# Weights in smaller loads, and a new order of stages, in an adaLN attention-and-GEGLU kernel

## The chip, the cores and the metric

The kernel runs on one core of one Trainium2 chip. The metric is the device time of one execution in microseconds (us). A profile of one execution, taken by the hardware profiler, goes with each kernel; the times in it are microseconds from the start of its span.

A few names that the profile uses: PE is TensorE (matmuls), PEld its weight loads, DVE is VectorE, ACT is ScalarE, POOL is GpSimd and SP is SyncE, which here only issues transfers. "SPq" is SP's queue of transfer issues. L681 is line 681 of the kernel.

## What is computed

One transformer block with adaptive layer norm, for 2048 tokens of width 512, in bfloat16:

```python
mod = (silu(c) @ w_mod)                      # six rows of 512: sa, ca, ga, sb, cb, gb
h = layernorm(x) * (1 + ca) + sa
x = x + ga * A(h, wqkv, wo)                  # attention
h = layernorm(x) * (1 + cb) + sb
x = x + gb * ((gelu(h @ w_gate) * (h @ w_up)) @ w_down)    # width 1792 inside
```

The attention has 32 heads of width 16. A token sees 8 tokens: itself and those 2, 4, ... 14 places before it. The softmax is over these eight.

## The kernel before

**Tiling.** The tokens go through in five groups, `GROUPS`: two of 256 tokens and three of 512. For each group the stages are: layer norm and transposition into `hT` (`ln1`), the projections to Q, K and V (`emit_qkv`, matmuls at L681, copies out of PSUM at L704), attention (`emit_attention`), a second layer norm into `h2T`, and the feed-forward part (`emit_ffn`, gate and up matmuls at L945, down matmuls at L971). The feed-forward of a group is emitted after the attention of the next one.

**Attention without a score matrix.** Q times the shifted K is an elementwise product on VectorE (`pq`, L764), which a narrow matmul folds over a head's width into `LT` (L776). The maximum over the eight is found on VectorE (`Lb`, L797 to L819) and subtracted by a matmul (L824). Exp on ScalarE gives `e` (L831). Two matmuls with the constant F1 sum `e` over the eight places into `ss` (L839). ScalarE turns the sum into its reciprocal by Ln and Exp (L844, L845), and VectorE multiplies (L848). `e` times the shifted V is again a product on VectorE (`pv`, L860 and L866), folded by matmuls into `o_ps` (L879). The shifted V comes from memory: V is stored to a scratch tensor (`scr`, L708) and read back shifted as `vR` (four transfers for each tile, L725). The output projection with `woP` is at L904. VectorE has multiplied `woP` by the row ga once, at L999, after all four of its loads, and `WdP` by gb at L1002.

**Loads.** All large loads are issued from SP. `load_rows` cuts a weight into `cuts` transfers of equal size; before the change w_gate (`Wg`), w_up (`Wu`) and w_down (`WdP`) come in two halves each. `load_wqkv` loads a third of wqkv; wq comes in two halves, wk and wv whole. The first group's K projection is written in two steps for each PSUM tile, rows 0 to 255 of wk and then rows 256 to 511; in the built program both tiles take their first step before either takes its second.

**What sets the order.** No order is written out by hand. Every operation is recorded with an engine, an estimated time, the tiles that it reads and writes, and a priority from the table `PRI`. `Plan.order` then places operations one by one: of those that are ready, it takes the one with the earliest start by its own estimate of times, and among equals the lowest priority. `Plan.MARGIN` adds a margin for each engine, `Plan.AHEAD` holds loads back that are not urgent, and `Plan.SKEW` adds to the estimated end of a transfer in a long run of transfers. `emit` writes the instructions in the order so found, and each engine runs its own in that order. So a change of a number in `PRI` can move instructions on any engine.

Each transfer is given one of eight completion counters in turn, and an issue on SP waits until the transfer eight places before it is complete.

Of the kernel before, what the change touches and what calls it, by code (L numbers as in the profile page):

```python
# [8 lines left out]
ACT = mybir.ActivationFunctionType  # L9
ALU = mybir.AluOpType  # L10
AX = mybir.AxisListType
F32 = mybir.dt.float32
# [6 lines left out]
def _ap(base, free_dims, offset=0):  # L19
    return bass.AP(base.tensor, base.offset + offset, [list(base.ap[0])] + [list(d) for d in free_dims])  # L20
# [164 lines left out]
class Engines:  # L185
    def __init__(self, nc, pl):
# [14 lines left out]
MERGE = (3, 4)  # L201
FMERGE = 0
DVEMAX = (4,)
CUT = 384
XB1 = {4: "act"}
XB2 = {1: "act", 2: "act", 3: "act", 4: "act"}
PRI = {
        "mod0": 3.1,
        "ln1": (-1825.3, -1417, -559.1, -142.2, 405),
        "qkv": (-441.8, 155.6, 232.8, 131.6, 1308),  # L210
        "att": (-554.3, 44.5, -1074.5, 462.1, 1752.4),
        "ffn": (1196.5, 2593, 2774.3, 2477.6, 1886.7),
        "glu": (5.6, 211.5, -2302.6, 838.6, 2147),
        "mod": (-159.3, -303.9, 262.1),
        "wo": 1823,
        "wd": 1171.4,
        "scr": -3307.9,
        "vR": -3609.4,
        "warm": (5, 6, 0, 3),
        "load": {"wk": -997.5, "wv": -995.5, "x1": -997.86, "x2": -995.23, "wm2": -1001.63, "wo": -878.5, "x3": -1000.04,  # L220
        "wm3": -994.66, "wm4": -996.59, "x4": -995.73, "Wg": -868.86, "Wu": -870.61, "wm5": -855.38, "Wd":
        -862.75},
}
Plan.MARGIN = {"pe": 0.48, "act": -0.15, "dve": 0.16, "pool": -1.48, "sp": 0.37}
Plan.AHEAD = 2.07
Plan.SKEW = 2.6
Plan.TURN = 0


# [1 line left out]
def kernel(  # L231
# [13 lines left out]
    nc = tc.nc  # L245
    P = 128
    S, D = 2048, 512
    H, DH, W = 32, 16, 8
    F = 1792
    SG = 512  # L250
    DT = D // P
# [42 lines left out]
    F1 = ctile([P, P], BF16, "F1")  # L294
# [109 lines left out]
    def load_rows(t, src, p, cuts, rows):  # L404
        n = len(t.shape) and t.shape[1] // cuts
        for i in range(cuts):
            dma(1835e3 / cuts, lambda i=i: nc.sync.dma_start(
                out=t[:, i * n:(i + 1) * n, :],
                in_=src[i * n * P:(i + 1) * n * P, :].rearrange(rows, p=P)),
                w=[(t, k) for k in range(i * n, (i + 1) * n)], pri=p + 0.1 * i, bw=385e3)  # L410

    L = PRI["load"]
# [3 lines left out]
        w=[wm01], pri=-999, bw=390e3)  # L416

    def load_wqkv(b, p, cuts=1):
        m = DT // cuts
        for i in range(cuts):  # L420
            dma(524e3 / cuts, lambda i=i: nc.sync.dma_start(
                out=wqkv[b][:, m * i:m * i + m, :],
                in_=A_wqkv[m * i * P:m * (i + 1) * P, b * D:(b + 1) * D].rearrange("(o p) n -> p o n", p=P)),
                w=[(wqkv[b], k) for k in range(m * i, m * i + m)], pri=p + 0.02 * i)

    load_wqkv(0, -998.65, 2)
    load_wqkv(1, L["wk"])
    load_wqkv(2, L["wv"])
    load_x(2, 4, L["x1"])
    load_x(4, 8, L["x2"])  # L430
# [1 line left out]
    for d4 in range(4):  # L432
        dma(131e3, lambda d4=d4: nc.sync.dma_start(
            out=woP[32 * d4:32 * d4 + 32, :, :],
            in_=bass.AP(A_wo.tensor, A_wo.offset + 4 * D * d4, [[16 * D, H], [D, 4], [1, D]])), w=[(woP, d4)],
            pri=L["wo"], bw=250e3)
# [1 line left out]
    load_wm(wm3, 3, L["wm3"])  # L438
    load_wm(wm4, 4, L["wm4"])
    load_x(12, 16, L["x4"])  # L440
    load_rows(Wg, B_w_gate, L["Wg"], 2, "(dt p) f -> p dt f")
    load_rows(Wu, B_w_up, L["Wu"], 2, "(dt p) f -> p dt f")
    load_wm_halves(wm5, 5, L["wm5"])
    load_rows(WdP, B_w_down, L["Wd"], 2, "(dt p) f -> p dt f")

    wps = T("psF", [P, SG], F32, "warm_ps")

# [20 lines left out]
    def sigmoid():  # L468
# [6 lines left out]
        w=[scT], pri=-2000)  # L475
# [72 lines left out]
    mod0 = []  # L548
# [108 lines left out]
    q, hT, vR = {}, {}, {}  # L657
# [56 lines left out]
    def emit_attention(g):  # L714
        tok0, n = GROUPS[g]
# [5 lines left out]
        for i, t in enumerate(vR[g]):  # L721
            rs = [(scr, (gg, i if GROUPS[gg][1] == SG else 0)) for gg in range(max(g - 1, 0), g + 1)]
            for r in (0, 2, 1, 3):
                queue, on = (nc.scalar, E.dma_act) if r in SECOND else (nc.sync, dma)
                on(32 * 4 * njv * (n + 8) * 2, lambda r=r, t=t, i=i, queue=queue: queue.dma_start(  # L725
                    out=t[32 * r:32 * r + 32, :, :, :].rearrange("p a b c -> p (a b) c") if njv == 4
                    else t[32 * r:32 * r + 32, :, :, :],
                    in_=bass.AP(scr.t.tensor, scr.t.offset + 2 * i * ROW + tok0 + 2 + 2 * r,
                                [[16 * ROW, H], [ROW, 16], [1, n + 8]] if njv == 4 else
                                [[16 * ROW, H], [4 * ROW, 4], [ROW, 2], [1, n + 8]])),  # L730
                    r=rs, w=[(t, r)], pri=PRI["vR"] + 0.1 * g, bw=330e3 if SECOND else 205e3)
# [25 lines left out]
        for jj in range(steps):  # L757
            p = base + jj
            pq = products("pq", jj)
            pqs.append(pq)  # L760
            for m in range(4):
                j, wg = (2 * jj + m // 2, m % 2) if n == SG else (m, 0)
                no = 4 if n == SG else 8
                dve(1.145, lambda j=j, wg=wg, no=no, t=pq[m]: nc.vector.tensor_tensor(  # L764
                    out=t[:], in0=_ap(q[g][:, j, :], [[0, no], [1, n]]),
                    in1=_ap(kT[:, j, :], [[2, no], [1, n]], offset=tok0 + HALO - (6 + 8 * wg if no == 4 else 14)),
                    op=ALU.mult), r=[(q[g], j)] + kd(j), w=[pq[m]], pri=p)
# [14 lines left out]
        p = base + 5  # L782
# [9 lines left out]
        e = T("e", [P, 2, n], BF16, "e")  # L792
        for b in range(nb):
            act(act_us(SG), lambda b=b: nc.scalar.copy(out=Lb[:] if nb == 1 else Lb[:, b:b + 1, :], in_=LT[b][:]),
                r=[LT[b]], w=[(Lb, b)], pri=p - 1000)
        us = 0.072 + n * 0.52e-3
        dve(us, lambda: nc.vector.tensor_tensor(out=Lb[:, 0, :], in0=Lb[:, 0, :], in1=Lb[:, 1, :], op=ALU.max),  # L797
            r=[Lb], w=[Lb], pri=p)
        if g in DVEMAX:
# [12 lines left out]
            for b, t in enumerate(LT):  # L812
                dve(0.072 + SG * 2 // nb * 1.041e-3, lambda t=t: nc.vector.tensor_tensor(
                    out=t[:], in0=t[:], in1=_ap(all4[:], [[0, 2 // nb], [1, n]]), op=ALU.subtract), r=[t, all4], w=[t],
                    pri=p)
        else:
            dve(us, lambda: nc.vector.tensor_tensor(out=Lb[0:64, 1, :], in0=Lb[0:64, 0, :], in1=Lb[64:128, 0, :],
                                                    op=ALU.max), r=[Lb], w=[Lb], pri=p)
            dve(us, lambda: nc.vector.tensor_tensor(out=Lb[0:32, 0, :], in0=Lb[0:32, 1, :], in1=Lb[32:64, 1, :],  # L819
                                                    op=ALU.max), r=[Lb], w=[Lb], pri=p)  # L820
# [11 lines left out]

        act(act_us(SG) * nb, exps, r=LT, w=[e], pri=p - 1000, table="exp")

        ss = T("psB", [P, n], F32, "ss")

        def sums():
            for wg in range(2):
                nc.tensor.matmul(ss[:], lhsT=F1[:], rhs=e[:, wg, :], start=(wg == 0), stop=(wg == 1))  # L839

        pe(2 * MM * n / SG, sums, r=[F1, e], w=[ss], pri=p, pad=ss)

        def invert():
            nc.scalar.activation(out=ss[:], in_=ss[:], func=ACT.Ln)  # L844
            nc.scalar.activation(out=ss[:], in_=ss[:], func=ACT.Exp, scale=-1.0)  # L845

        act(2 * act_us(n) + 0.1, invert, r=[ss], w=[ss], pri=p - 1000, table="exp")
        dve(0.072 + 2 * n * 1.041e-3, lambda: nc.vector.tensor_tensor(  # L848
            out=e[:], in0=e[:], in1=_ap(ss[:], [[0, 2], [1, n]]), op=ALU.mult), r=[e, ss], w=[e], pri=p)

        oT = T("oT", [P, 4, SG], BF16, "oT")
        pvs = []
        for jj in range(steps):
            p = base + 6 + jj
            pv = products("pv", jj)
            pvs.append(pv)
            if n == SG:
                for m in range(4):
                    jl, wg = m // 2, m % 2
                    dve(1.145, lambda jj=jj, jl=jl, wg=wg, t=pv[m]: nc.vector.tensor_tensor(  # L860
                        out=t[:], in0=_ap(e[:, wg, :], [[0, 4], [1, n]]),
# [25 lines left out]
        p = base + 11  # L887
# [150 lines left out]
```

## Time and profile before

| what | us |
|---|---|
| median of 5 runs | 243.18 (242.39 to 243.86) |
| the profiled execution | 242.39 |
| its span | 240.4 |
| TensorE busy | 233.9 (97% of the span) |
| VectorE busy | 160.9 |
| ScalarE busy | 159.2 |
| GpSimd busy | 13.9 |

The loads before the first use of w_gate come in one stream: 28.23 MB go through the queues in all, and the first 52 us hold most of the loads. For single transfers, the time line of SP gives the moment of the issue, and the view of transfers gives the time from issue to landing:

| transfer | issued | to landing |
|---|---|---|
| wk, 512 KB | 3.67 | 7.1 |
| wv, 512 KB | 4.20 | 8.1 |
| woP, the first of four, 128 KB | 14.00 | 8.6 |
| scr store of the first group, 272 KB | 16.82 | 7.3 |
| Wu, first half, 896 KB | 19.04 | 8.2 |
| Wu, second half, 896 KB | 20.66 | 10.8 |
| vR of the first group, the first of four, 264 KB | 24.10 | 8.4 |

Busy time is not a bound by itself: an engine that is busy for most of the span can still wait in the stretch that matters. The view of waits tells for each engine what it sat idle for, and the chain that ended last follows the end of the kernel back from wait to wait.

### The profile page before, as it was taken

The numbers are of one execution on the slowest core, as the hardware profiler recorded it, in microseconds if no ns is written. First come the engines' busy times: TensorE is split into PE (matmuls) and PEld (weight loads), VectorE is DVE, ScalarE is ACT, GpSimd is POOL, SyncE is SP. The second block draws the span as 40 slices with busy tenths as digits, with TensorE's granted clock in tenths as the row PEclk, the third lists the DMA queues.
The fourth block names the chain that finished last, engine by engine and source line by source line (L and its number), as shares of the span: only waits on it lengthen the run. The fifth ranks groups of instructions, "written<-read, shape, count | busy, mean of one in ns | idle before, by whom it ended". The sixth has DMA issues, their size and how long they took to land.

```text
span 240.4 us, 4190 instructions
## 1 busy us (share of the span) xinstructions
PE 233.9 (97%) x1588; PEld 126.1 (52%) x1588; DVE 160.9 (67%) x307; ACT 159.2 (66%) x298; POOL 13.9 (6%) x35
## 2 busy tenths in 40 slices
PE   7899899999999999999999999999999999999994
PEld 2798445567674557664444444444444444444442
DVE  4689869849997799981899897489455122222222
ACT  4388797699696878669866676846767801666400
POOL 6000240100001000020000002000011000000000
PEclk9999999999999999999999999999999999999999
DMA  6999999999842139412129404100003010000011
GB/s 212 362 366 336 302 276 350 231 279 218 215 75 44 44 81 255 111 35 56 44 55 214 89 3 78 53 22 26 0 1 73 17 44 21 22 0 3 0 44 44
DMA packets 34917, 28.23 MB, mean 117 GB/s; under 512 B 10961, under 2 KB 33234, under 8 KB 34898
## 3 DMA queue, kind: packets, MB, share of 16 engines
q1 hardware_dynamic: 34896, 27.97, 46.0%
q8 instruction: 12, 0.20, 0.4%
q14 instruction: 7, 0.06, 0.1%
q10 hardware_dynamic: 2, 0.00, 0.0%
HBM read 21.40 MB, written 4.21 MB: 107 GB/s over the span
## 4 chain that ended last, share of the span: by engine, by line
PE 86%; DVE 6%; DMA 3%; ACT 2%; SPq 1%; issue 1%; DVEq 0%
PE u_ps L945 20%; PE g_ps L945 20%; PE y_ps L971 20%; PE qkv_ps L681 12%; PE x_ps L904 6%; PE o_ps L879 3%; DMA wk<-in_A_wqkv_dram 3%; PE LT L776 3%; DVE st L620 2%; DVE pq L764 2%; ACT hT L551 1%; DVE xn L536 1%; PE ss L839 1%; PE LT L824 1%; DVE x_sg L979 1%
## 5 line engine op out<-in xcount | busy, mean ns | idle before, releaser
L945 PE MATMUL g_ps<-h2T,Wg 128*128 128x512 bf16 (+1 forms) x280 | 57.7, 337 | 0.0
L945 PE MATMUL u_ps<-h2T,Wu 128*128 128x512 bf16 (+1 forms) x280 | 57.7, 337 | 0.0
L971 PE MATMUL y_ps<-WdP,hht 128*128 128x512 bf16 (+2 forms) x238 | 50.3, 367 | 0.0
L954 ACT ACTIVATE gl<-g_ps 128x512 bf16<-128x512 f32 x56 | 33.5, 598 | 23.8 <-PE g_ps L945 18.9
L958 DVE TENSOR_TENSOR hht<-gl,ub 128x512 bf16<-128x512 bf16 x56 | 23.3, 421 | 31.0 <-ACT ub L957 30.8
L957 ACT CAST ub<-u_ps 128x512 bf16<-128x512 f32 x56 | 32.8, 586 | 15.4 <-PE u_ps L945 15.4
L945 PEld LDWEIGHTS <-Wg 128*128 128x128 bf16 x280 | 27.1, 98 | 23.3 <-issue 1.7
L945 PEld LDWEIGHTS <-Wu 128*128 128x128 bf16 x280 | 27.1, 98 | 22.2 <-issue 1.3
L764 DVE TENSOR_TENSOR pq<-qT,kT 128x2048 bf16<-128x2048 bf16 x32 | 38.0, 1216 | 0.9 <-ACT kT L704 0.9
L971 PEld LDWEIGHTS <-hht 128*128 128x128 bf16 x238 | 22.7, 98 | 25.9 <-issue 0.4
L860 DVE TENSOR_TENSOR pv<-e,vR 128x2048 bf16<-128x2048 bf16 x24 | 28.3, 1217 | 0.1
L979 DVE TENSOR_TENSOR x_sg<-y_ps,x_sg 128x512 bf16<-128x512 f32 (+2 forms) x17 | 10.8, 657 | 26.1 <-PE y_ps L971 26.1
L541 POOL TENSOR_TENSOR rstd<-rstd,neghalf 128x2 f32<-128x2 f32 x12 | 9.8, 821 | 168.3 <-DVE rstd L919 107.0
L681 PE MATMUL qkv_ps<-hT,wq 128*128 128x512 bf16 (+1 forms) x80 | 16.5, 336 | 0.7 <-ACT hT L551 0.6
L681 PE MATMUL qkv_ps<-hT,wk 128*128 128x512 bf16 (+1 forms) x80 | 16.4, 337 | 0.8 <-DMA wk<-in_A_wqkv_dram 0.8
L681 PE MATMUL qkv_ps<-hT,wv 128*128 128x512 bf16 (+1 forms) x80 | 15.5, 337 | 0.0
L904 PE MATMUL x_ps<-woP,oT 128*128 128x512 bf16 x64 | 15.3, 379 | 0.0
L911 ACT ACTIVATE xn<-x_sg 128x512 bf16<-128x512 bf16 x16 | 10.0, 628 | 4.1 <-DVE x_sg L908 3.9
L704 ACT CAST kT<-qkv_ps 128x512 bf16<-128x512 f32 x16 | 9.4, 593 | 4.3 <-PE qkv_ps L681 4.2
L681 PEld LDWEIGHTS <-wk 128*128 128x128 bf16 x80 | 8.7, 114 | 5.8 <-DMA wk<-in_A_wqkv_dram 1.0
L620 DVE BATCH_NORM_STATS2 st<-x_sg 128x6 f32<-128x512 bf16 x16 | 10.2, 680 | 2.2 <-DMA x_sg<-in_A_x_dram 2.2
L681 PEld LDWEIGHTS <-wq 128*128 128x128 bf16 x80 | 8.8, 114 | 5.3 <-issue 1.2
(100 smaller groups left out, 217.9 us busy)
## 6 DMA issues: line engine op xcount, KB each, us to landing
vR<-scr SPq DMA_DIRECT2D x24, 260.0 KB, 5.2
vR<-scr SPq DMA_DIRECT2D x8, 264.0 KB, 9.0
out_dram<-x_sg SPq DMA_DIRECT2D x15, 128.0 KB, 1.7
Wu<-in_B_w_up_dram SPq DMA_DIRECT2D x2, 896.0 KB, 9.5
scr<-vT SPq DMA_DIRECT2D x7, 256.0 KB, 7.7
Wg<-in_B_w_gate_dram SPq DMA_DIRECT2D x2, 896.0 KB, 7.6
WdP<-in_B_w_down_dram SPq DMA_DIRECT2D x2, 896.0 KB, 9.7
x_sg<-in_A_x_dram SPq DMA_DIRECT2D x3, 512.0 KB, 8.8
```

What stands on the lines that cost most here:

```text
L620: stats = lambda i=i, st=st, tok=tok: nc.vector.bn_stats(out=st[:, i, :], in_=xrow(tok + P * i))
L681: nc.tensor.matmul(shaped(ps[:, jl, :], g, XB1), lhsT=wqkv[b][:, dt, j + jl:D:4], rhs=columns(hT[g], g, dt, XB1), start=(dt == 0 and (jl = ...
L764: dve(1.145, lambda j=j, wg=wg, no=no, t=pq[m]: nc.vector.tensor_tensor(out=t[:], in0=_ap(q[g][:, j, :], [[0, no], [1, n]]), in1=_ap(kT[:, ...
L860: dve(1.145, lambda jj=jj, jl=jl, wg=wg, t=pv[m]: nc.vector.tensor_tensor(out=t[:], in0=_ap(e[:, wg, :], [[0, 4], [1, n]]), in1=vR[g][jj][ ...
L904: nc.tensor.matmul(x1_ps[:], lhsT=oT[:, j, c4 * P:(c4 + 1) * P], rhs=woP[:, j, :], start=(j == 0), stop=(j == 3))
L911: act(0.7, lambda i=i, tok=tok, xn=xn, sq=sq: nc.scalar.activation(out=xn[:, i, :], in_=xrow(tok), func=ACT.Square, scale=D ** -0.5, accum ...
L945: nc.tensor.matmul(shaped(ps[:, f, :], g, XB2), lhsT=Wt[:, dt, ft * P:(ft + 1) * P], rhs=columns(h2[g], g, dt, XB2), start=(dt == 0), stop ...
L954: act(act_us(SG), lambda gl=gl, ps=gu[0]: nc.scalar.activation(out=gl[:], in_=flat(ps), func=ACT.Gelu_apprx_tanh), r=[gu[0]], w=[gl], pri= ...
L957: act(act_us(SG), lambda ub=ub, ps=gu[1]: nc.scalar.copy(out=ub[:], in_=flat(ps)), r=[gu[1]], w=[ub], pri=p)
L958: dve(0.339, lambda gl=gl, ub=ub, ht=hh[u // 2], u=u: nc.vector.tensor_tensor(out=ht[:, u % 2, :], in0=gl[:], in1=ub[:], op=ALU.mult), r=[ ...
L971: nc.tensor.matmul(y_ps[:], lhsT=hh[u // 2][:, u % 2, f * n + c4 * P:f * n + (c4 + 1) * P], rhs=WdP[:, ft, lo_d:hi_d], start=(ft == 0), st ...
L979: dve(0.07 + nd * 1.041e-3, lambda y_row=y_row, y_ps=y_ps: nc.vector.tensor_tensor(out=y_row(), in0=y_ps[:], in1=y_row(), op=ALU.add), r=[ ...
```

## The change

wk arrives in two halves, w_gate and w_up in quarters, and the numbers of the planner are others. A new switch, `DVESUM`, would make the softmax sum of a group on VectorE in place of the two matmuls; it is empty, so no group uses it, and that part of the diff is cut here.

```diff
+DVESUM = ()
+WCUT = (4, 2)
...
-        "mod0": 3.1,
-        "ln1": (-1825.3, -1417, -559.1, -142.2, 405),
-        "qkv": (-441.8, 155.6, 232.8, 131.6, 1308),
-        "att": (-554.3, 44.5, -1074.5, 462.1, 1752.4),
-        "ffn": (1196.5, 2593, 2774.3, 2477.6, 1886.7),
-        "glu": (5.6, 211.5, -2302.6, 838.6, 2147),
-        "mod": (-159.3, -303.9, 262.1),
-        "wo": 1823,
-        "wd": 1171.4,
-        "scr": -3307.9,
-        "vR": -3609.4,
+        "mod0": 673.7,
+        "ln1": (-1746.8, -1406.1, -598.2, -62.7, 630.2),
+        "qkv": (-381.3, 151, 275.4, 147.9, 1324.9),
+        "att": (-554.3, -5.9, -1074.5, 604.6, 1636.2),
+        "ffn": (1214.9, 2614.9, 2774.3, 1995.3, 1991.7),
+        "glu": (-11.4, 214.5, -2060.3, 887.3, 2172.5),
+        "mod": (-304, -394.9, 455.9),
+        "wo": 1366.7,
+        "wd": 1024.1,
+        "scr": -3014,
+        "vR": -3603.1,
...
-        "load": {"wk": -997.5, "wv": -995.5, "x1": -997.86, "x2": -995.23, "wm2": -1001.63, "wo": -878.5, "x3": -1000.04,
-        "wm3": -994.66, "wm4": -996.59, "x4": -995.73, "Wg": -868.86, "Wu": -870.61, "wm5": -855.38, "Wd":
+        "load": {"wk": -997.5, "wv": -995.5, "x1": -997.86, "x2": -993.39, "wm2": -1001.63, "wo": -872.67, "x3":
+        -1000.04, "wm3": -989.07, "wm4": -995, "x4": -995.73, "Wg": -868.86, "Wu": -988.57, "wm5": -851.3, "Wd":
         -862.75},
...
-Plan.MARGIN = {"pe": 0.48, "act": -0.15, "dve": 0.16, "pool": -1.48, "sp": 0.37}
-Plan.AHEAD = 2.07
-Plan.SKEW = 2.6
+Plan.MARGIN = {"pe": 0.51, "act": -0.23, "dve": 0.16, "pool": -0.68, "sp": 0.4}
+Plan.AHEAD = 1.88
+Plan.SKEW = 2.48
...
-    load_wqkv(1, L["wk"])
+
+    def load_wk():
+        for i in range(2):
+            nc.sync.dma_start(out=wqkv[1][:, 2 * i:2 * i + 2, :],
+                              in_=A_wqkv[2 * i * P:2 * (i + 1) * P, D:2 * D].rearrange("(o p) n -> p o n", p=P))
+
+    dma(524e3, load_wk, w=[(wqkv[1], k) for k in range(DT)], pri=L["wk"])
...
-    load_rows(Wg, B_w_gate, L["Wg"], 2, "(dt p) f -> p dt f")
-    load_rows(Wu, B_w_up, L["Wu"], 2, "(dt p) f -> p dt f")
+    load_rows(Wg, B_w_gate, L["Wg"], WCUT[0], "(dt p) f -> p dt f")
+    load_rows(Wu, B_w_up, L["Wu"], WCUT[0], "(dt p) f -> p dt f")
...
-    load_rows(WdP, B_w_down, L["Wd"], 2, "(dt p) f -> p dt f")
+    load_rows(WdP, B_w_down, L["Wd"], WCUT[1], "(dt p) f -> p dt f")
```

The planner records wk as one load of 524 KB, though it is issued as two transfers. In the order that the planner makes of the new numbers, four things differ from before:

- SP: wk in two; the four loads of woP stand behind the four quarters of Wu instead of in front of its halves, and the first scr store stands behind the first quarter of Wu; Wg in four. The rest of SP's order is the same.
- ScalarE: the pair L844, L845 of the first group stands ahead of the second of four modulates of `hT` (L551) instead of behind it.
- TensorE: one K projection of four matmuls (L681, near 72 us) stands ahead of the first eight matmuls of y_ps (L971) instead of behind them.
- VectorE and GpSimd have the same instructions in the same order.

More of the change, by code (lines that the diff above doesn't have):

```diff
@@ L833, in emit_attention @@
         act(act_us(SG) * nb, exps, r=LT, w=[e], pri=p - 1000, table="exp")
[L835 to L845, printed above, removed]
@@ L847, in emit_attention, with spread_sums, invert, sums @@
-        act(2 * act_us(n) + 0.1, invert, r=[ss], w=[ss], pri=p - 1000, table="exp")
-        dve(0.072 + 2 * n * 1.041e-3, lambda: nc.vector.tensor_tensor(
-            out=e[:], in0=e[:], in1=_ap(ss[:], [[0, 2], [1, n]]), op=ALU.mult), r=[e, ss], w=[e], pri=p)
+        if g in DVESUM:
+            add = lambda out, a, b: nc.vector.tensor_tensor(out=out, in0=a, in1=b, op=ALU.add)
+            s1, s2, s3 = [T("prod", [P, n], F32, "s%d" % k) for k in range(3)]
+            def spread_sums():
+                for r in range(4):
+                    add(s3[32 * r:32 * r + 32, :], s2[0:32, :], s2[32:64, :])
+            dve(0.6, lambda: add(s1[:], e[:, 0, :], e[:, 1, :]), r=[e], w=[s1], pri=p)
+            dve(0.6, lambda: add(s2[0:64, :], s1[0:64, :], s1[64:128, :]), r=[s1], w=[s2], pri=p)
+            dve(2.4, spread_sums, r=[s2], w=[s3], pri=p)
+            def invert():
+                nc.scalar.activation(out=s3[:], in_=s3[:], func=ACT.Ln)
+                nc.scalar.activation(out=s3[:], in_=s3[:], func=ACT.Exp, scale=-1.0)
+            act(2 * act_us(n) + 0.1, invert, r=[s3], w=[s3], pri=p - 1000, table="exp")
+            dve(0.072 + 2 * n * 1.041e-3, lambda: nc.vector.tensor_tensor(
+                out=e[:], in0=e[:], in1=_ap(s3[:], [[0, 2], [1, n]]), op=ALU.mult), r=[e, s3], w=[e], pri=p)
+        else:
+            ss = T("psB", [P, n], F32, "ss")
+            def sums():
+                for wg in range(2):
+                    nc.tensor.matmul(ss[:], lhsT=F1[:], rhs=e[:, wg, :], start=(wg == 0), stop=(wg == 1))
+            pe(2 * MM * n / SG, sums, r=[F1, e], w=[ss], pri=p, pad=ss)
+            def invert():
+                nc.scalar.activation(out=ss[:], in_=ss[:], func=ACT.Ln)
+                nc.scalar.activation(out=ss[:], in_=ss[:], func=ACT.Exp, scale=-1.0)
+            act(2 * act_us(n) + 0.1, invert, r=[ss], w=[ss], pri=p - 1000, table="exp")
+            dve(0.072 + 2 * n * 1.041e-3, lambda: nc.vector.tensor_tensor(
+                out=e[:], in0=e[:], in1=_ap(ss[:], [[0, 2], [1, n]]), op=ALU.mult), r=[e, ss], w=[e], pri=p)
```

## The prediction

> **What bounds the kernel now.** I read the page's busy shares first, then TensorE's own waits, then the chain that ended last, then the time lines of the stretch where the chain leaves TensorE.
>
> ```profile
> PE 233.9 (97%) x1588; PEld 126.1 (52%) x1588; DVE 160.9 (67%) x307; ACT 159.2 (66%) x298; POOL 13.9 (6%) x35
> PEclk9999999999999999999999999999999999999999
> ```
>
> TensorE is busy for 97% of the span at the full granted clock, so what the change can win or lose lies in TensorE's few gaps. The view of waits, for TensorE alone, has four lines:
>
> ```profile
> PE warm_ps L450 <- DVE one L320: 1.3, 1, 1.3
> PE qkv_ps L681 <- DMA wk<-in_A_wqkv_dram: 0.8, 1, 0.8
> PE LT L824 <- DVE Lb L819: 0.7, 1, 0.7
> PE qkv_ps L681 <- ACT hT L551: 0.6, 2, 0.4
> ```
>
> Only the second is a load that the change touches. The chain, in order of time (start, length, what), says how far that wait is felt:
>
> ```profile
> 3.67 7.14 DMA wk<-in_A_wqkv_dram
> 10.86 1.51 PE qkv_ps L681 x12
> 12.40 0.59 ACT kT L704
> 13.08 1.23 DVE pq L764
> 14.31 2.38 DVE st L620 x4
> ...
> 29.14 1.35 ACT hT L551 x2
> 30.50 0.28 ACT ss L844
> 30.80 0.37 ACT ss L845
> 31.17 1.36 ACT hT L551 x2
> 32.58 7.07 PE qkv_ps L681 x32
> 39.64 0.99 PE o_ps L879 x32
> ```
>
> The reader is to see three things: wk sets the start of the chain (landed 3.67 + 7.14 = 10.81); from 13.08 to about 27 VectorE carries it; from 32.58 on it is TensorE without a gap up to the last addition at 236.2. A gain at the front must pass VectorE, then the ScalarE stretch at 29 to 32.6, and then the first fold of attention products, o_ps at 39.6, whose inputs come from VectorE:
>
> ```profile
> 29.60 0.38 PE L839 MATMUL ss<-e,F 128*128 128x256 bf16 x2
> 30.11 1.23 DVE L999 TENSOR_TENSOR woP<-woP,wide 128x2048 bf16<-128x2048 bf16 x1
> 30.24 2.45 POOL L541 TENSOR_TENSOR rstd<-rstd,neghalf 128x2 f32<-128x2 f32 x2 [4.06 <-DVE rstd L632]
> 35.45 4.63 DVE L866 TENSOR_TENSOR pv<-e,vR 128x2048 bf16<-128x2048 bf16 x4 [1.55 <-DMA vR<-scr]
> ```
>
> The last of the four pv products ends at 40.08; the matmuls that need it (the last eight of o_ps) start at 40.24 in the trace's records. So there is only about 0.1 us between "vR landed at 35.3" and "TensorE waits".
>
> **The change, part by part.** The two programs' instruction orders show that VectorE and GpSimd keep their order completely. What differs is below.
>
> (1) wk in two halves. The kernel's first K projection takes eight matmuls on rows 0 to 255 for both of its PSUM tiles, then eight on rows 256 to 511; now the first eight wait for the first half alone. Neighbours in the same queue show the price of a half: wq's two halves of 256 KB landed 0.75 us apart, the x load behind them 0.77 later, wk (512 KB) 1.50 after that. So the first half should land 0.75 earlier, at 10.06. TensorE has just then finished wq (0.75 idle in the waits). Eight matmuls take 8 x 0.109 = 0.87, to 10.98, when the second half (10.81) is there. The twelfth matmul, which releases the first kT copy, comes 0.75 earlier: kT copy at 11.65, pq at 12.33 instead of 13.08. VectorE is free at 12.21, so pq can start. But it then ends at 13.48, and the next instruction, st L620, needs the third x load, which lands at 13.82 (wv lands 1.5 after wk, this load 1.5 after wv). st starts at 13.85 instead of 14.23: **0.38 of the 0.75 survives.** VectorE's queue is then full to 27, and all it waits for in between moves with it; TensorE's wait for Lb L819 (26.92) moves too. Term: -0.38.
>
> The rule that speaks against this: the Trainium skill, "DMA: Bandwidth & Descriptors", § Anatomy of one DMA, gives each transfer a fixed 2.0 us (mostly the write receipt) besides bytes over 436 GB/s, and its rules for authors say to coalesce (the fit is for the path issued from GpSimd; these come from SP). Added in full, the second half would land 2.0 + 0.6 = 2.6 after the first, at 12.7: pq some 1.9 late and the sum an estimated +1.8. The row says 0.75 from half to half[...]. I take the row, with 0.02 to 0.05 for each extra transfer.
>
> (2) ScalarE: the pair Ln, Exp on ss (L844, L845) moves ahead of one modulate of hT (L551). Before, the two modulates start at 29.04 and 29.72, L844 at 30.38 without waiting. The sums ss leave TensorE at 29.60 + 0.38 = 29.98. Now L844 stands at the slot of 29.72 and must wait to about 30.01. Then the spacings of before: L845 0.42 later, the next modulate 0.28 after it (30.71), then 31.38 and 32.04, against 31.74: the fourth modulate ends 0.30 later. qkv_ps at 32.58 needs the buffer that this modulate frees (its 0.42 wait). Queued behind on ScalarE are the K and Q copies, 0.4 ahead of need. Term: **+0.30.** Everything here shifts together with term (1), so both count: TensorE starts its gapless stretch 0.08 earlier.
>
> (3) Wu in quarters, ahead of woP. SP's queue was woP, woP, scr store, woP, woP, Wu, Wu, vR x4; it is now Wu, scr store, Wu x3, woP x4, vR x4. The load queue is saturated here (DMA share 1.0 or more in every 2 us window from 8 to 52), so places are bytes. woP moves behind 1.8 MB and lands last before vR, about where Wu's second half landed, 20.66 + 10.8 = 31.5. VectorE's L999 (30.11) waits for all of woP: a stall of about 1.8 (it starts 1.4 later than before). Queued behind it are rstd L632, xn L536, e L848, xn L536 and then pv, which itself waited 1.55 for vR. Before, these ran from 31.25 to 33.9. Afterwards L999 ends near 32.7, then 0.65 (xn), 0.6 (e), 0.65 (xn): 34.6. pv still waits for vR at 35.3: **hidden, with 0.6 to spare**; if woP came later than 32.1 it would cost microsecond for microsecond.
>
> Here a second rule counts: the Trainium skill, "SBUF — State Buffer", § SBUF: two separate sides, says that GpSimd and a VectorE instruction with two SBUF inputs take one port pair in turns, for a whole instruction. The row fits: the two pow at 30.24 took 2.45 beside L999, two others at 24.53 and 25.45 took 0.71 and 0.73. So the first pow, now done while VectorE stalls, gets shorter; the second may be blocked by xn or e for up to 0.7, which makes 34.6 into 35.3 at worst: still no cost. By the row 34.6, by the rule up to 35.3; I use 34.6.
>
> (4) scr and vR. The scr store is now behind one quarter (448 KB) instead of two pieces of woP (256 KB): 192 KB at the 346 GB/s of 22 to 26 us are 0.55, so it lands near 24.65. vR's first issue waited for it (at 24.10). But ahead of vR in the transfer queue lie the same bytes as before, to 31.5, so issuing 0.5 later is hidden. The build gives transfers eight completion counters in turn, so vR's second to fourth issues wait for the Wu quarters, the last at about 29, two microseconds or more before its turn. What remains is three more transfers than before: 3 x 0.02 to 0.05, x = +0.06 to +0.15 on vR. Bounds: -0.4 (woP's 4 KB rows, 240 GB/s when mixed with the scr store, may go faster) to +1.2 (the last vR issued late). I take +0.1. TensorE arrives 0.08 earlier with 0.1 of slack: **+0.08.**
>
> (5) At no cost: Wg in quarters (Wg landed by 40.7, used at 52.94; 12 us cover), five more issues on SP of about 0.5 each (SP waits in this stretch; what is behind it, Wg and Wd, has that same cover), and on TensorE the swap of one K projection with two y_ps groups at 72 (twelve matmuls of 0.216 in either order; the next waiter, LT L824 at 74.62, stays in place, and its Lb was done at 74.0; y_ps starts later, so its own inputs have more time). The new branch for sums on VectorE is built for no group.
>
> Sum: -0.38 + 0.30 + 0.08 = 0.0 on the span of 240.4. The profiled execution took 242.39, 2.0 more than its span, and is the fastest of the five; their median is 243.18, 0.8 above. So I forecast **243.1**, no change.
>
> **The rivals.** *The front gain survives*: vR comes 0.3 earlier, or ScalarE waits less for ss. For it: VectorE and the fold have nothing else late. Against it: terms (1) and (2) cap it at -0.38, or -0.75 if the x load came earlier too, which no row suggests: about 242.7. *vR late, slower*: place is the fold o_ps at 39.6; every microsecond that vR lands after 35.4 is a microsecond on the end, since TensorE is gapless afterwards. At +0.83, landing at 36.1, it is 0.3% slower; at the bound of +1.2, 244.3. For it: issues now hang on landings of Wu quarters. Against it: same bytes ahead, in a full queue. *The halves don't help*: both land at 10.8; then terms 0 + 0.30 + 0 give 243.5.
>
> **How the numbers follow.** About 0.3% (0.73 us) is what a measurement of this kernel can tell from no change. Chances: forecast 0.55, front gain 0.15, halves useless 0.08, vR late 0.22. Forecast and useless halves are almost all within the limit; of the front gain's 0.15 some 0.09 pass it (with the medians' own spread of a few tenths), of vR late some 0.17. Faster 0.10, same 0.70, slower 0.20. Range: the forecast's own is 242.6 to 243.7; with the other cases 242.4 to 244.3.
>
> **What would show it.** Right: kT's first wk matmul near 10.1; st L620 waiting for an x load until 13.85; a new ScalarE wait of 0.3 at L844; L999 waiting for woP to 31.5 with pv still near 35.4; TensorE gapless from about 32.5. Wrong: pv starting past 36 or before 35, L999 past 32.1, or a new TensorE wait after 40.

## The result, and the profile after

The changed kernel takes **242.19 us** in the median of 43 runs (241.69 to 244.19), the kernel before, run beside it, 242.92 in 80 runs (241.99 to 245.64). The ratio is 0.9971 with a 95% interval of 0.9961 to 0.9982: faster by 0.3%. The forecast was no change, 243.1 in a range of 242.4 to 244.3.

The profiled execution took 242.18, with a span of 240.1; before it was 242.39 and 240.4. So the two profiles differ by 0.2 to 0.3 us, and the medians by 0.7. Most of the gain isn't in this pair of profiles, and that is what the experiments are about.

The busy shares of the page, and TensorE's waits (us in total, times, longest):

```profile
PE 233.6 (97%) x1588; PEld 125.7 (52%) x1588; DVE 160.9 (67%) x307; ACT 159.4 (66%) x298; POOL 12.9 (5%) x35
...
PEclk9999999999999999999999999999999999999999
```

```profile
...
PE qkv_ps L689 <- ACT hT L559: 0.7, 3, 0.3
PE LT L832 <- DVE Lb L827: 0.6, 1, 0.6
PE tp L573 <- DVE xn L544: 0.5, 2, 0.3
PE qkv_ps L689 <- DMA wv<-in_A_wqkv_dram: 0.3, 1, 0.3
```

The wait of 0.8 for wk is gone; 0.3 for wv and 0.5 for xn have come, and one more wait for hT. The chain that ended last, in order of time:

```profile
5.40 8.24 DMA x_sg<-in_A_x_dram
13.67 2.47 DVE st L628 x4
...
30.22 2.03 ACT hT L559 x3
32.29 7.07 PE qkv_ps L689 x32
39.36 1.01 PE o_ps L907 x32
```

It no longer begins with wk but with the x load that the prediction named as the next one late. From 32.29 on TensorE has no gap, as before from 32.58. Two places on TensorE, one ahead of this stretch and one at its end, mark the path: the matmul on `Lb` and the first fold of attention products, `o_ps`. Before and after:

```profile
26.92 0.38 PE L824 MATMUL LT<-Lb,NB 128*128 128x512 bf16 x1 [0.71 <-DVE Lb L819]
...
39.57 1.06 PE L879 MATMUL o_ps<-pv,F 128*32 128x256 bf16 x32
```

```profile
26.36 0.38 PE L832 MATMUL LT<-Lb,NB 128*128 128x512 bf16 x1 [0.56 <-DVE Lb L827]
...
39.29 1.08 PE L907 MATMUL o_ps<-pv,F 128*32 128x256 bf16 x32
```

The first comes 0.56 earlier, the second 0.28: that is the whole difference of the two spans. The time line of the stretch between, for ScalarE, TensorE, GpSimd and VectorE:

```profile
29.03 0.38 PE L867 MATMUL ss<-e,F 128*128 128x256 bf16 x2
...
29.45 0.37 ACT L872 ACTIVATE ss<-ss 128x256 f32<-128x256 f32 x1 [0.19 <-PE ss L867]
...
29.68 0.69 POOL L549 TENSOR_TENSOR rstd<-rstd,neghalf 128x2 f32<-128x2 f32 x1 [4.05 <-DVE rstd L640]
...
30.40 1.23 DVE L1027 TENSOR_TENSOR woP<-woP,wide 128x2048 bf16<-128x2048 bf16 x1 [0.86 <-DMA woP<-in_A_wo_dram]
...
31.85 0.72 POOL L549 TENSOR_TENSOR rstd<-rstd,neghalf 128x2 f32<-128x2 f32 x1 [1.48 <-DVE rstd L640]
...
35.28 4.63 DVE L894 TENSOR_TENSOR pv<-e,vR 128x2048 bf16<-128x2048 bf16 x4 [1.70 <-DMA vR<-scr]
```

The moved pair waits 0.19 for ss; VectorE waits 0.86 for woP and yet stands 1.70 idle ahead of pv, for vR. The signs of being right that the prediction listed are all there, near the places it gave them except for woP, which is in at 30.40 and not at 31.5; none of its signs of being wrong is. What is not in this profile is a reason for 0.7 us.

### The profile page after: what moved, and what is told of

Its sections match the earlier page's. It is cut to its first block, busy times and chain, and to the rows that moved or that the text cites. A ratio compares the mean times of both kernels' runs of the same rounds, so it can differ in the third digit from the quotient of the medians.

```text
span 240.1 us, 4193 instructions
## 1 busy us (share of the span) xinstructions
PE 233.6 (97%) x1588; PEld 125.7 (52%) x1588; DVE 160.9 (67%) x307; ACT 159.4 (66%) x298; POOL 12.9 (5%) x35
## 4 chain that ended last, share of the span: by engine, by line
PE 86%; DVE 5%; DMA 3%; SPq 2%; ACT 1%; issue 1%; DVEq 0%
PE u_ps L973 20%; PE g_ps L973 20%; PE y_ps L999 20%; PE qkv_ps L689 12%; PE x_ps L932 6%; DMA x_sg<-in_A_x_dram 3%; PE o_ps L907 3%; PE LT L784 3%; DVE st L628 2%; DVE pq L772 1%; ACT hT L559 1%; DVE xn L544 1%; PE ss L867 1%; SPq L423 1%; PE LT L832 1%
## 5 line engine op out<-in xcount | busy, mean ns | idle before, releaser
L549 POOL TENSOR_TENSOR rstd<-rstd,neghalf 128x2 f32<-128x2 f32 x12 | 8.8, 732 | 169.0 <-DVE rstd L947 106.9
L605 ACT ACTIVATE h2T<-h2T,modT,scl 128x512 bf16<-128x512 bf16 (+1 forms) x16 | 11.0, 752 | 2.1 <-DMA h2T<-xn 2.1
L628 DVE BATCH_NORM_STATS2 st<-x_sg 128x6 f32<-128x512 bf16 x16 | 10.2, 680 | 2.7 <-DMA x_sg<-in_A_x_dram 2.7
```

Of the source, the lines that this page charges most:

```text
L605: act(act_us(n, 2), lambda dt=dt: nc.scalar.activation(out=dst[:, :, dt, :], in_=dst[:, :, dt, :], func=ACT.Identity, scale=scl[:, off // ...
L628: stats = lambda i=i, st=st, tok=tok: nc.vector.bn_stats(out=st[:, i, :], in_=xrow(tok + P * i))
```

## The experiments

Three theories. **A**: the gain is the front's, the wk halves less the moved pair of ScalarE, and the difference between 0.3 and 0.7 is noise. **B**: in most of its runs, other than the profiled one, the kernel before lands its first vR late and TensorE waits at the first o_ps; the change's order of loads takes that wait away. **C**: the medians differ because other runs fell on a lower granted clock. Each median below is of one chip with the kernel before beside it; the kernel before stood at 242.92, 242.72, 242.56, 242.73, 242.98 and 242.35 from one chip to the next, so small differences are read within a chip, in traces, or in runs of several chips together. Line numbers are each kernel's own.

**e1: the kernel before, unchanged, profiled again.**

> The kernel before, unchanged, a second time. The question is what of the 0.3 us between the two profiled spans (240.4 and 240.1) and of the 0.7 us between the medians belongs to the change at all. In the first profile of it the third x load landed at 13.8 and vR at 35.3; in that of the changed kernel 13.6 and 35.2, although the transfers up to wm were the same, so a part of that can be chance. If landings vary by some 0.2 us from run to run, theory A (a fixed gain at the front) expects span 240.4 +- 0.4 and a ratio of 1.000. Theory B (vR lands late in most runs of the kernel before, and the profiled one was a lucky run) expects vR at 35.6 or later here and a wait of TensorE at the first o_ps, span 240.8 or more. Theory C (the medians differ by runs at a lower granted clock) expects spans of 241.4 or more at a clock of 0.99 in a good part of the runs and 240.4 in the others.

243.32 (22 runs), ratio 1.0022 (1.0004 to 1.0039). The same kernel against itself is thus 0.2% off, more than its interval says. Its median is 0.60 above that of the same program on the same chip (242.72 in 67 runs), and no run shows why. So a difference of this size between two medians is no proof by itself in what follows; traces, and counts over several chips, have to carry it. The second profile (span 240.9) has what the first lacks:

```profile
36.01 4.63 DVE L866 TENSOR_TENSOR pv<-e,vR 128x2048 bf16<-128x2048 bf16 x4 [2.31 <-issue]
...
39.38 0.84 PE L879 MATMUL o_ps<-pv,F 128*32 128x256 bf16 x24
...
40.70 0.40 PE L879 MATMUL o_ps<-pv,F 128*32 128x256 bf16 x8 [0.48 <-DVE pv L866]
```

TensorE came to o_ps 0.19 sooner than in the first profile, and left it 0.47 later: pv began at 36.01 and not at 35.45, because vR's last share landed at 35.84 instead of 35.27 (the trace's records of landings). The view puts pv's wait down to "issue", but its vR operand is what had just landed.

**e2: wk in halves as the one change on the kernel before.** The orders of all engines but SP's are those of before.

```diff
-    load_wqkv(1, L["wk"])
...
+    dma(524e3, load_wk, w=[(wqkv[1], k) for k in range(DT)], pri=L["wk"])
```

> The kernel before with wk in two halves and nothing else; every engine keeps its order. Theory A, the front: the first K matmul at 10.0, st L620 0.4 to 0.55 us earlier, and without the new ScalarE wait TensorE could be 0.4 to 0.55 earlier at 32.6; but the last pv product (vR at 35.3) then holds the first o_ps for 0.2 to 0.4. Net -0.15 to -0.3 us, ratio 0.9990. Theory B, that the changed kernel wins by the order of the later loads: no more than -0.1, ratio 0.9996 or more.

243.27 (22 runs), ratio 1.0017 (0.9993 to 1.0041): no gain, and theory A falls in that form. The profile shows that the front gain was made and taken back:

```profile
37.17 4.63 DVE L872 TENSOR_TENSOR pv<-e,vR 128x2048 bf16<-128x2048 bf16 x4 [3.86 <-DMA vR<-scr]
...
38.98 0.40 PE L885 MATMUL o_ps<-pv,F 128*32 128x256 bf16 x8
39.58 0.40 PE L885 MATMUL o_ps<-pv,F 128*32 128x256 bf16 x8 [0.20 <-DVE pv L872]
...
40.72 0.40 PE L885 MATMUL o_ps<-pv,F 128*32 128x256 bf16 x8 [0.73 <-DVE pv L872]
41.85 0.40 PE L885 MATMUL o_ps<-pv,F 128*32 128x256 bf16 x8 [0.73 <-DVE pv L872]
```

TensorE is at o_ps 0.59 sooner than before (38.98 against 39.57), then waits 1.66 for pv, and the span is 242.0.

**e3 and e4: the changed kernel with wk whole, and with ScalarE's pair back behind the second modulate.** `inv0` is that pair, in the list that the planner has placed.

```diff
...
-    dma(524e3, load_wk, w=[(wqkv[1], k) for k in range(DT)], pri=L["wk"])
+    load_wqkv(1, L["wk"])
```

```diff
...
+        i = placed.index(self.inv0)
+        j = next(k for k in range(i + 1, len(placed)) if placed[k].eng == "act")
...
+        placed.insert(j, placed.pop(i))
```

> The changed kernel with wk in one transfer again, all else as changed. Theory A: no front gain is left, and the ScalarE wait of 0.2 to 0.3 us for the sums stays: +0.2 to +0.3 against the kernel before, ratio 1.0010, first K matmul at 10.8. Theory B: most of the gain stays, ratio 0.998 or less.

> The changed kernel with the pair Ln, Exp of the first group back behind the second modulate, as before; all else as changed. Theory A: the wait of ScalarE for the sums (0.19 us) is gone and the qkv group at 32.3 starts 0.25 to 0.3 earlier, at 32.0; but vR (35.2) does not come earlier, so the first o_ps waits for pv about as long, and the end gains 0 to 0.1 against the changed kernel: ratio to the kernel before 0.9968 to 0.9972. If vR were not the limit: 0.996.

e3: 242.52 (22 runs), ratio 0.9990 (0.9967 to 1.0014). This lies between A's 1.0010 and B's 0.998, so the time decides little; in e3's profile vR's last share landed at 34.43, pv began at 34.56, and TensorE didn't wait for it, which is B's picture. e4: 242.28 (14 runs), 0.9975 (0.9950 to 1.0000): without its wait on ScalarE the changed kernel is no faster (0.9971, on another chip). Both fit a cap behind the front, as in B; neither shows it.

**e5 and e6: both kernels without the wait for the first vR.** All transfers are still issued, in the same order.

```diff
-                        in1=_ap(vR[g][0][:], [[-8, 2], [njv * (n + 8), 4], [1, n]], offset=j * (n + 8) + 8),
+                        in1=_ap(xs[3][:], [[-8, 2], [D, 4], [1, n]], offset=64 * j + 8) if g == 0 else
+                        _ap(vR[g][0][:], [[-8, 2], [njv * (n + 8), 4], [1, n]], offset=j * (n + 8) + 8),
```

> The kernel before, in which the first group's four pv products read a part of x that landed long ago in place of the spread V rows (vR); every transfer, the load of vR too, is still issued and in the same order, so only the wait is gone, and the values of the first group's attention output are not the reference's. Theory B (what holds the kernel before back in most of its runs is that the first vR lands late and TensorE then waits for pv at the first o_ps): pv starts at 33.9 (35.45 less the 1.55 that it waited in the profile) instead of 35.45 to 37.2, TensorE never waits for pv at the first o_ps, and the median goes down to where the fastest quarter of its runs lies, 242.1 to 242.4, from about 242.9 to 243.3: ratio 0.997 +- 0.001; runs over 242.8 at a granted clock of 1.0, which are nearly half of the kernel before's, become rare. Theory A (the gain of the change is the front alone) and theory C (chance and clock): the median stays at the kernel before's, ratio 1.000 to 1.002.

> The changed kernel with the same edit: the first group's pv products read a part of x and not vR, so their values are not the reference's. The front gain of the change (first K matmul at 9.9 and not 10.86, Lb 0.56 earlier) is now met by no vR. Theory B: 241.8 to 242.1, 0.1 to 0.3 below the changed kernel, since vR lands so that TensorE is just not held at the first o_ps there; against the kernel before without the wait it keeps the front gain of 0.2 to 0.4. If theory A's front gain were all of it, this kernel would stand 0.6 to 0.8 below the kernel before without the wait.

e5: 242.21 (22 runs), ratio 0.9986 (0.9974 to 0.9999). e6: 242.06 (22 runs), 0.9978 (0.9969 to 0.9987). e5's median is where B put it; its ratio is nearer to 1 than B's 0.997 because the kernel before stood at only 242.56 on this chip. e6 keeps only 0.15 of the front's gain against e5, where 0.2 to 0.4 was expected; e13 to e16 take that up. In e5's profile pv no longer waits, and o_ps runs through:

```profile
33.54 4.62 DVE L866 TENSOR_TENSOR pv<-e,x_sg 128x2048 bf16<-128x2048 bf16 x4
...
39.30 1.06 PE L880 MATMUL o_ps<-pv,F 128*32 128x256 bf16 x32
```

The single runs show it best. Of all runs with a granted clock of at least 0.997, counted over all chips after the first comparison (for which the kernel before's clocks are not listed), the kernel before took over 242.8 us in 65 of 203 (in 49 of 182 if e1's are left out), without the vR wait (e5, e9) in 2 of 32; the changed kernel, with its first comparison, in 1 of 59. No profile caught one of the kernel before's runs over 242.8 (e1's was of a run of 242.71). That these runs waited for vR is inferred from their near absence once the wait is taken out. Theory C doesn't account for the difference: a clock under 0.997 fell on 23 of 226 runs of the kernel before and on 8 of 67 of the changed one, and the counts above are of the other runs.

**e7 and e8: which edit brings vR forward?** On the kernel before, e7 puts the two halves of Wu ahead of woP (Wu, scr, Wu, woP x4, vR x4); e8 cuts Wu and Wg into quarters and keeps woP ahead. Nothing else moves on any engine. In e7's diff, `early_wu` and `late_wo` are the loads of Wu and woP, and `scr0` is the first scr store.

```diff
+        first = [o for o in placed if o in self.early_wu] + [o for o in placed if o in self.late_wo]
+        for o in first:
+            placed.remove(o)
+        i = placed.index(self.scr0)
+        placed[i:i + 1] = [first[0], self.scr0] + first[1:]
```

```diff
-    load_rows(Wg, B_w_gate, L["Wg"], 2, "(dt p) f -> p dt f")
-    load_rows(Wu, B_w_up, L["Wu"], 2, "(dt p) f -> p dt f")
+    load_rows(Wg, B_w_gate, L["Wg"], 4, "(dt p) f -> p dt f")
+    load_rows(Wu, B_w_up, L["Wu"], 4, "(dt p) f -> p dt f")
```

> The kernel before with one thing of the change alone: its two halves of Wu go ahead of woP on SP's queue (Wu, scr, Wu, woP in four, vR), wk whole, no quarters; the orders of the other four engines are the ones of before. If it is the order that brings vR in (theory B1): vR's last share lands at 34.6 to 35.2, pv starts by 35.3, TensorE doesn't wait for it at the first o_ps, median 242.3 to 242.5, ratio 0.998. If it is the quarters (B2): vR's last share at 35.8 to 37, a wait of 0.5 to 1.7 at the first o_ps, median 243 or above, ratio 1.000 to 1.002. Theory A: 1.000 in either case.

> The kernel before with one thing of the change alone: Wu and Wg in quarters of 448 KB and not halves, woP still ahead of Wu, wk whole; the orders of the other engines are the ones of before. If it is the quarters (theory B2): the slowest share of Wu lands less far behind its fellows (31.45 behind a first at 27.19 in the kernel before), vR's last share at 34.4 to 35.2, no wait at the first o_ps, median 242.3 to 242.5, ratio 0.998. If it is the order (B1): vR's last share at 35.8 or later and a median of 242.9 to 243.3, ratio 1.000 to 1.002. Theory A: 1.000.

e7: 242.36 (22 runs), ratio 0.9989 (0.9980 to 0.9998). e8: 243.07 (14 runs), 1.0018 (1.0002 to 1.0033). At full clock, as counted above, e8 took over 242.8 in 8 of 13 runs, but e7 and e11 (below), which have Wu first and no quarters, in 2 of 32. **The order does it, not the quarters.** e7's time line:

```profile
35.21 4.63 DVE L877 TENSOR_TENSOR pv<-e,vR 128x2048 bf16<-128x2048 bf16 x4 [1.04 <-DMA vR<-scr]
```

e8's profile has vR at 35.30 and no wait; it is of the fastest of its 14 runs (242.21), and none of the others was traced. The landings in all profiles with vR behind both weights:

| order on SP | profiles | last share of the last vR lands at | mean | mean of its 16 shares |
|---|---|---|---|---|
| woP, then Wu, then vR | before, e1, e2, e5, e8, e9, e10, e16 | 35.27 to 36.99 | 36.05 | 33.90 |
| Wu, then woP, then vR | after, e3, e4, e6, e7, e11, e12, e14, e15, e18 | 34.43 to 35.67 | 35.06 | 33.35 |

A transfer lands in 16 shares, and its reader waits for the last. With the same bytes ahead of it vR comes a microsecond sooner when woP and not Wu is next ahead: about half because all shares come sooner, half because the last of the 16 is less far behind the others. The two rows don't hold the same mix of kernels; with wk whole the means are 35.7 (five profiles) and 34.7 (two), with wk in halves 36.7 (three) and 35.1 (eight). The gap stands in both, and the single profiles overlap.

**e9 and e10: the halves of wk alone, with no vR behind them.** The edits of e5 and of e2 and e5 together.

> The kernel before without the wait for the first vR once more (the first group's pv products read a part of x, so their values are not the reference's), as the base for the next one on the same chip: 242.2 by theory B, as it was the first time (242.21), and 0.3 to 0.7 below the kernel before wherever that one stands on this chip.

> wk in two halves as the one thing of the change, on the kernel before without the wait for the first vR (so the values of the first group's attention are not the reference's). Now nothing behind the front takes its gain back. If the front gain of the halves is what the prediction had for it, 0.38, the median is 241.8 and the ratio to the last kernel 0.9984; if it is what the starts of the first LT in the traces so far say (21.09 to 21.36 with wk whole, 20.91 and 20.94 with halves: 0.25 in the mean), 241.95 and 0.999; if the front gain is absorbed before the end (a planned pause of TensorE, the wait on hT), 242.2 and 1.000.

e9: 242.06 (12 runs), ratio 0.9978 (0.9959 to 0.9997). e10: 241.71 (7 runs), 0.9942 (0.9917 to 0.9968). On one chip the halves gain **0.35** when vR cannot take it back: theory A's mechanism with close to the prediction's size of 0.38. The same two kernels over all chips, at full clock: 242.15 (e5, e9; 32 runs) and 241.82 (e10, e16; 15 runs).

**e11 and e12: halves and Wu first alone, and the changed kernel again.** e11 has the edits of e2 and of e7.

> The kernel before with the two parts of the change that the runs point to and nothing else: wk in two halves, and Wu, in its two halves, ahead of woP. The orders of the other four engines are the ones of before, so the pair of table functions of the first group stands behind the modulate, and there are no quarters. Theory B: vR's last share lands by 35.1, no wait at the first o_ps or one under 0.3, median 242.0 to 242.3, the changed kernel's own within 0.15. If the quarters or the moved pair of ScalarE earn something of their own, it stands 0.2 or more above the changed kernel.

> The changed kernel once more, for its time on the same chip as the last three and for a second profile. 242.2 by theory B, with runs that lie as close together as the first time (nine in ten within 241.8 and 242.6 where the granted clock is 1.0). The second profile tells how much of the 0.56 by which the first one's Lb stood ahead of the kernel before's was that run: the first K matmul at 9.9 to 10.3 and LT's first matmul at 20.9 to 21.3. No wait over 0.3 at the first o_ps.

e11: 242.36 (12 runs), 0.9987 (0.9966 to 1.0008). e12: 242.31 (12 runs), 0.9992 (0.9971 to 1.0012). e11 needs neither quarters nor the moved pair for the changed kernel's time, and doesn't beat it: its TensorE is at o_ps at 39.35, earlier than e12's 39.59, but there the 32 matmuls take 1.38 instead of 1.06, since pv started only at 35.65.

**e13 to e16: vR forward in another way; what the moved pair costs.** Still open was where the front gain goes in the changed kernel. e13 is e2 with Wu's second half behind the first vR; e14 is e4, e15 the changed kernel and e16 e2, each without the vR wait. In e13's diff, `wu` is the load of Wu's second half and `vr0` the last of the first vR's four.

```diff
+        placed.remove(self.wu)
+        placed.insert(placed.index(self.vr0) + 1, self.wu)
```

> The kernel before with wk in two halves, and with the second half of Wu behind the first vR's four loads on SP's queue (woP, scr, woP, first half of Wu, vR in four, second half of Wu); all orders of the other engines are the ones of before, and the whole is computed. Theory B: vR has 896 KB less ahead of it, some 2.4 us of landings, so that its last share lands at 32.5 to 33.5, pv starts at 33.4 to 33.9 without a wait of over 0.3 on vR, TensorE doesn't wait at the first o_ps, Wu's second half lands by 36.5, long before the first u_ps at 53.8, and the median is that of the halves without the wait for vR: 241.7 to 241.9, ratio 0.995 to 0.997, and 0.4 below the changed kernel. If something else than vR also takes the gain: 242.1 or above.

> The changed kernel with ScalarE's pair of table functions of the first group back behind the second modulate, and without the wait for the first vR (so the first group's attention values are not the reference's). If the pair costs the 0.30 that the prediction had for it, 241.7 to 241.8, 0.2 to 0.35 below the next kernel; if the pair costs nothing and the quarters or the swapped products hold the changed kernel back, the same as the next one within 0.1.

> The changed kernel without the wait for the first vR once more (so the first group's attention values are not the reference's), on the same chip as the kernel ahead of it and the one behind: 242.06, as the first time, within 0.1.

> The halves of wk alone on the kernel before without the wait for the first vR once more (so the first group's attention values are not the reference's): 241.7 to 241.8, as the first time (241.71 in only 7 runs); the same within 0.1 as the changed kernel with the pair back, if the quarters and the swapped products are worth nothing.

e13: 241.91 (7 runs), ratio 0.9958 (0.9938 to 0.9978). e14: 241.80 (6), 0.9956 (0.9936 to 0.9976). e15: 241.99 (7), 0.9960 (0.9944 to 0.9976). e16: 241.92 (8), 0.9955 (0.9938 to 0.9971). In e13 vR's last share lands at 33.16, and pv doesn't wait for it:

```profile
33.34 4.63 DVE L878 TENSOR_TENSOR pv<-e,vR 128x2048 bf16<-128x2048 bf16 x4
...
39.06 1.06 PE L891 MATMUL o_ps<-pv,F 128*32 128x256 bf16 x32
```

The medians of e14, e15 and e16 are of too few runs for 0.1 or 0.2; the traces are sharper. From the start of the matmul on Lb (L824 before) to the start of o_ps it is 12.64 or 12.65 in each of the fourteen profiles with the pair in its old place, but 12.93 or 12.94 in each of the six with the pair moved (after, e3, e6, e12, e15, e18). **The moved pair costs 0.28**, by this wait of TensorE for hT in e12

```profile
31.26 1.02 PE L689 MATMUL qkv_ps<-hT,wk 128*128 128x512 bf16 x4 [0.23 <-ACT hT L559]
32.60 1.02 PE L689 MATMUL qkv_ps<-hT,wq 128*128 128x512 bf16 x4 [0.32 <-ACT hT L559]
```

against a single one of 0.42 in e13.

**e17 and e18: e13 beside the changed kernel on one chip.**

> The kernel before with wk in two halves and the second half of Wu behind the first vR once more: 241.9, as the first time, 0.3 to 0.4 below the changed kernel on the same chip by theory B; 0.1 or less below it if the first time was the chip.

> The changed kernel beside it on the same chip: 242.2 to 242.3.

e17: 241.91 (12 runs), ratio 0.9980 (0.9957 to 1.0003). e18: 242.27 (11 runs), 0.9988 (0.9967 to 1.0008). The changed kernel thus gains only 0.08 on the kernel before here, which took over 242.8 in only 2 of its 21 runs at full clock on this chip: where vR seldom comes late, there is little to mend. And e13's kernel stands 0.36 below the changed one on this chip. That pair has no interval of its own, but at full clock the middle half of e13's and e17's runs lies in 241.69 to 242.00, that of the changed kernel's in 242.04 to 242.34. Of the kernels here that compute the whole it is the fastest.

## Why the prediction was wrong, point by point

One regularity makes the sum simple. In all twenty profiles what follows the first o_ps is the same: from the first instruction behind it on TensorE to the end of the span it is 199.8 to 200.0 (240.4 - 40.56 before, 240.1 - 40.30 after, 242.0 - 42.19 in e2). All that these kernels differ by is decided ahead of 41 us.

1. **wk in halves, -0.38: right.** The first K matmul went from 10.86 to 9.93 (10.1 was forecast), st L628 waits 0.29 for the x load and starts at 13.67 (13.85). The profiled pair shows 0.56 at the matmul on Lb (26.92 to 26.36), but some of that is the run: with wk whole that start varies from 26.48 to 26.92 in seven profiles, with halves from 26.21 to 26.71 in twelve (e17, told of at the end, left out). The means, 26.75 and 26.43, are 0.32 apart, and the medians of e9 and e10 0.35. The two halves landed 0.74 apart in the profile after (9.88 and 10.62), so it was right to take the row, and not the fixed 2.0 us that the Trainium skill, "DMA: Bandwidth & Descriptors", § Anatomy of one DMA, gives each transfer (fitted there for transfers issued from GpSimd).
2. **ScalarE's pair, +0.30: right,** 0.28 by the spacings above.
3. **woP behind Wu, hidden: right,** though the stall was put too high. L1027 starts at 30.40, not 31.5, VectorE waits 0.86 for woP and not about 1.8, and pv waits 1.70 after it. The second pow was not held up beside xn and e (0.72).
4. **vR, +0.1 and so +0.08: this step failed, in sign and size.** It said that "ahead of vR in the transfer queue lie the same bytes as before", and from that a vR later by the price of three transfers. The bytes are the same, but vR's last share lands 1.0 earlier in the mean of the profiles (0.1 in the profiled pair, 35.27 to 35.16). The start of vR had the wrong sign too: its first issue was to come after a scr store that lands near 24.65, and came at 23.54 (24.10 before). The last issue came at 28.45 (26.11 before), late as forecast, and this load still landed no later. The lower bound of -0.4 allowed for some of it; it was then worth nothing in the sum, because the profiled execution showed TensorE just not waiting for vR.
5. **No cost of the quarters and the swap: right** so far as 0.1 can be told (e14 241.80 with them, e16 241.92 without, on one chip). Nor are the quarters of use (e8).

The second half of the same error is the step from the profile to the median: "their median is 243.18, 0.8 above. So I forecast 243.1". The 0.8 was carried over as a constant. Some of it was the small sample: 80 runs have 242.92, which is 0.26 of the 0.9 by which the forecast is too high. For the rest, the profiled execution was the fastest of five, and what slower ones have more of is in the main no overhead: it goes when the wait for vR at o_ps is taken out (0.48 of wait in e1's profile). By medians at full clock over all chips: before 242.59, without the wait 242.15, the changed kernel without the wait 242.05, the changed kernel 242.20. So the kernel before lost about 0.44 to vR and the changed one about 0.15; this 0.29 and the 0.10 that the front keeps make the difference of 0.39. The chips behind the four medians are not the same, and none of the three profiles of the changed kernel (after, e12, e18) shows a wait for pv at o_ps, so the 0.15 is argued and not shown. Single comparisons scatter about it: 0.73 in the first, 0.42 with e12 and 0.08 with e18, the last two with 1 inside the interval of the ratio. How much of the first one's 0.73 is more than the 0.39 by chance is open.

The rivals: "vR late, slower" had the right place and the right mechanism, but was put to the wrong kernel: it held the one before, and the change mended it. "The front gain survives" had the sign and named an earlier vR as one of its two ways; with 242.7 it was still half a microsecond too high. "The halves don't help" is what e2 shows, though not for its reason: they helped, and vR took it back.

**Open**: why the order moves vR. Where woP is next behind the load wm4, the last share of wm4 already lands 1.5 to 2.6 behind the mean of the 16 (nine profiles); where a piece of Wu is next, 1.3 to 1.6 (ten). So the lag is there from the woP loads on, each of 128 KB to 32 partitions; whether their shape is the cause wasn't tried. Open too is why e1's runs stand 0.60 above those of the same program on the same chip.

## What to carry to other kernels

A profile is one run, and if it is the fastest of a few, ask what the others wait for before you add their distance as a constant: a slack of 0.1 us on a transfer whose landing varies by more is a wait in many runs. Take such a wait away by feeding its reader something that is already there; what that leaves tells what every other edit is worth. And of two gains on one path, first lift the one that ends last: here moving 896 KB that nobody needs before 53 us behind the read of vR turned the wk halves from no gain (e2, 1.0017) into the best kernel (e13, 0.9958, on another chip).

## What the runs showed of the hardware

- The order of the transfers changes when one lands that has the same bytes ahead of it: by 1.0 us in the mean of these profiles (36.05 against 35.06), in a stream that is full from 8 to 36 us (a DMA share of 1.01 or more in every 2 us of the profile before).
- With woP first, the wk halves made vR later: its last share at 36.16 to 36.99 (e2, e10, e16) against 35.27 to 36.11 (before, e1, e5, e9). One more transfer, 20 us earlier, and no fewer bytes; the cause is open.
- A run with a mean granted clock of 0.991 can have lost it in one place. e17's profile is such a run, beside e13's, the same kernel, in the view of windows (stretch, its length, busy time by engine, granted clock, share of the transfer engines, GB/s):

```profile
8.00:12.00 4.00, 3.96 (x40) 3.03 (x37) 3.15 (x9) 0.69 (x5) 0.00 (x0) 0.57 1.10 352
```

```profile
8.00:12.00 4.00, 3.85 (x40) 3.47 (x37) 3.40 (x11) 2.42 (x10) 0.00 (x0) 1.00 1.10 350
```

The clock was 0.57 for these 4 us and 1.00 around them; the 16 matmuls on wq took 3.37 instead of 1.91, the first K matmul came at 11.77 instead of 10.00, and the span was 1.4 longer. What set it off isn't shown; TensorE had been idle for 0.23 and 0.70 shortly before, in waits that e13's profile doesn't have; but the profile after has waits of 0.32 and 0.23 at about that place (5.88 and 6.51) and keeps its clock.
